# Attention feeding a gated MLP: the first stage ordered by a list scheduler, gate and value weights loaded once

## The chip, the cores and the metric

The kernel runs on one core of a Trainium2 chip. A core has five engines, each with its own instruction queue: TensorE (PE in the profile; its weight loads are PEld), VectorE (DVE), ScalarE (ACT), GpSimd (POOL) and SyncE (SP), which here issues the DMA transfers. The metric is the device time of one execution in microseconds, the median of several runs.

## The reference

```python
def sm_attn(qq, kk, vv):
    s = scale * np.matmul(qq, kk.transpose(0, 1, 3, 2))
    s = s - np.max(s, axis=-1, keepdims=True)
    a = np.exp(s)
    a = a / (np.sum(a, axis=-1, keepdims=True) + 1e-09)
    return np.matmul(a, vv)
q_d = q.reshape(B, H, Sd, factor, D).mean(axis=3)      # k_d, v_d likewise, factor = 4
out_up = np.repeat(sm_attn(q_d, k_d, v_d), factor, axis=2)
mask = np.abs(pos[:, None] - pos[None, :]) < factor
scores = np.where(mask, scale * np.matmul(q, k.transpose(0, 1, 3, 2)), -1000000000.0)
...                                                    # softmax of the scores, times v: out_local
x = (out_up + out_local).transpose(0, 2, 1, 3).reshape(B * S, H * D)
gate = 1.0 / (1.0 + np.exp(-(x @ w_gate)))
return gate * (x @ w_val) @ w_out
```

There are 8 batches of 8 heads, 576 positions and a head size of 64. The MLP has 4608 tokens, a model width of 512 and an inner width of 1536.

## The kernel before

**Attention.** Two heads of a batch form a unit, so there are 32 units, four to a batch. A unit loads four arrays (qk, qkd, v, vd), and its steps are: the pooled sums of q and k (prep2, GpSimd), the local scores s and the pooled scores sd (TensorE), their maxima, exponentials and sums, the transposes at and adt of the probabilities, their products with v (od for the pooled, x for the local part), and the sum of both, scaled (xs, VectorE), which is split into a high and a low half in f16 (xT, ScalarE and GpSimd). Units 0 to 7 (batches 0 and 1) keep their probabilities and v in f32, later units in f16 halves.

**MLP.** Tokens go in nine chunks of 512. For each of 12 slices of the inner width there is a gate product pg, a value product pv and an output product po, each of 12 matmuls of 128x512 in f16 (three products of halves for four pieces). A chunk needs the units of all its tokens: chunk 0 those of batch 0, chunk 1 those of batches 0 and 1.

**Weights.** They come as 64-bit words and are turned into two f16 halves on the chip. Each of 36 tiles (12 of each of wg, wv, wo, 512 KB each) is loaded twice. The first load (name ending in m) gives the absolute maximum (L160, VectorE), from which scales follow in two groups of slices; the second (ending in c) is converted in `wconv`: scaling on ScalarE (L213), a shift (L214), joining of the low bits (L215) and of the sign (L216) on VectorE, the high half on ScalarE (L222), the low half on GpSimd (L223). For wo both halves come from `split` (L164 ScalarE, L165 VectorE).

**Order.** The steps are put at positions by the numbers of the table `T`. Position 56 is the start of chunk 1; up to it the instructions are placed by the framework's scheduler in the order that its own estimates give, from there on TensorE keeps the order of the program. After that point a loop over chunks and slices issues gate, value and the output product of the slice before; a unit's steps are spread between them, and units are 9 positions (products) apart:

```python
    STEADY = dict(prep0=0, prep2=-3.5, s0=0, s1=0.1, sm=1.1, d0=2, dn=6.1, vd=9.4, v=8.2, a0=13, a1=13, at=14.4, od=15.6, x=16.6)
```

`awake` issues idle matmuls that keep TensorE active while it would wait. L413 is the line of every product, L491 the mask's addition to the local scores, L501 and L502 the maximum and its subtraction, L508 to L513 the sum and the division.

Of the kernel before, what the change touches and what calls it, by code (L numbers as in the profile page):

```python
# [19 lines left out]
T = dict(ma=4.5, mas=0.45, mb=9.5, mbs=0.5, c1=56, gs=2.66, g0=16.84, r1=1.99, rs=1.6, ob=3.16, v0=15.13, v1=16.62, v2=17.5, vs=2.12, o0=18, os=1.2, pro=2.36, u4=13.82, u5=21, u6=27, u7=32, l4=1.3, l5=2.77, l6=9.47, l7=8.68, lv=15.08, vm=1.58, b8=12, s8=9, hold=32.07, al=0.76, am=1, z=3.68, sd=0, sn=0.79, v0m=0.61, xd=[2, 3, 7], ad=[0, 3, 7], aa=[0, 1, 2, 3, 6], td=[0, 3, 9, 10], vd=[0, 1, 2, 3, 6, 9, 10], a_prep2=-0.89, a_s0=0.01, a_s1=0.52, a_sm=1.82, a_d0=2.39, a_dn=5.17, a_a0=4.37, a_vd=4.6, a_a1=5.1, a_v=2.74, a_at=5.22, a_od=5.79, a_x=8.38, m_prep0=-3.14, m_prep2=-1.43, m_s0=0.69, m_s1=2.59, m_sm=3.12, m_d0=2.84, m_a0=10, m_dn=10.78, m_vd=11.67, m_a1=12, m_v=13.07, m_at=13.44, m_od=15.64, m_x=17, k0=30, k_prep2=0, k_s0=2, k_s1=2, k_sm=4, k_d0=3, k_dn=0, k_a0=3, k_vd=8, k_a1=2, k_v=5, k_at=0, k_od=0, k_x=0)  # L20
# [22 lines left out]
TINY = 1e-30  # L43
EPS = 1e-9
NPC = NFC
WPC = DM
NWT = 1 + 2 * NPC
# [4 lines left out]
WAHEAD = 1  # L52
MAHEAD = 3
WGROUPS = [(0, 4), (4, NPC)]
SIGNBIT = -(1 << 31)
# [5 lines left out]
def attention_moe(ctx, tc, qk, qkd, v, vd, wg, wv, wo, mask, out):  # L61
# [23 lines left out]
    wg16 = cp.tile([P, NFC, 2, 4, P], F16, tag="wg16", name="wg16")  # L85
    wv16 = cp.tile([P, NFC, 2, 4, P], F16, tag="wv16", name="wv16")
# [7 lines left out]

    def borrow(i, n):
        taken[i] += n
        return room[i][:, NFC * WPC - taken[i] : NFC * WPC - taken[i] + n]

# [7 lines left out]
    def borrowed(eng, i, n):  # L106
        t = borrow(i, n * P)
        eng.memset(t, 0.0)
        return t.rearrange("p (a b) -> p a b", a=n)

    vplain = [borrowed(nc.vector, 0, NBLK), borrowed(nc.gpsimd, 0, NBLK)]
    vdblk = [zeroed(nc.gpsimd, [P, NKC, P], F32, f"vdblk{i}") for i in range(2)]
    ad = zeroed(nc.gpsimd, [QM, 2, NKC, 2, WIN], F32, "ad")
    vblk = cp.tile([P, 2, NBLK, P], F16, tag="vblk", name="vblk")
    flat = {id(vblk): vblk.rearrange("p t b c -> p (t b c)").bitcast(F32)}

    ones = cp.tile([P, 1], F32, tag="ones", name="ones")
# [781 lines left out]
```

## Time and profile before

| | |
|---|---|
| median of 3 runs | 1106.19 us (1105.46 to 1107.6) |
| profiled execution, its own time | 1106.37 us |
| its span | 1104.6 us |
| mean granted clock of TensorE | 0.956 |
| PE busy | 1047.4 us (95%) |
| DVE busy | 539.8 us (49%) |
| ACT busy | 476.6 us (43%) |
| POOL busy | 348.4 us (32%) |

The span runs from the first to the last instruction that the profile shows; the execution's own time is a little longer. Shares are means over the whole span; stages differ. The granted clock is given as a share of full speed (2.4 GHz).

### The profile page before, as it was taken

How to read it: one execution, taken by the hardware profiler on the slowest of the kernel's cores; microseconds unless marked ns; L12 is line 12 of the kernel's file. 1: busy time of each engine (PE TensorE's matmuls, PEld its weight loads, DVE VectorE, ACT ScalarE, POOL GpSimd, SP SyncE). 2: the span in 40 equal slices, each digit the busy share in tenths (PEclk: the TensorE clock that was granted, in tenths of full speed). 3: DMA queues.
4: the chain of work that ended last, by engine and by line, in shares of the span. 5: the costliest groups of instructions: out<-in, count | busy, mean ns of one | idle time of the engine just before them, and what ended most of it. 6: DMA issues, size and time to landing. Idle time of an engine off the chain costs nothing.

```text
span 1104.6 us, 18045 instructions
## 1 busy us (share of the span) xinstructions
PE 1047.4 (95%) x7267; PEld 546.4 (49%) x7267; DVE 539.8 (49%) x954; ACT 476.6 (43%) x1176; POOL 348.4 (32%) x348
## 2 busy tenths in 40 slices
PE   6877878988999999999999999999999999999998
PEld 4753334544555555555555555555555554444443
DVE  5779999855444444444444444444444322212112
ACT  5735566634444544454445444544444422122112
POOL 6424646633243334333433343333332200000000
PEclk8758989988999999999999999999999999999999
DMA  9977775422222322232223222321120000000001
GB/s 344 406 280 249 248 243 198 174 107 96 71 71 71 109 72 72 71 109 72 71 71 109 72 72 70 106 73 59 40 75 1 1 1 39 1 1 39 1 1 39
DMA packets 32083, 110.48 MB, mean 100 GB/s; under 512 B 3584, under 2 KB 3840, under 8 KB 32000
## 3 DMA queue, kind: packets, MB, share of 16 engines
q1 hardware_dynamic: 32000, 109.33, 28.4%
q8 instruction: 57, 0.93, 0.3%
q14 instruction: 26, 0.21, 0.1%
HBM read 99.88 MB, written 9.44 MB: 99 GB/s over the span
## 4 chain that ended last, share of the span: by engine, by line
PE 85%; DVE 7%; ACT 2%; DMA 2%; POOL 2%; issue 1%; SPq 0%; DVEq 0%; ACTq 0%
PE po L413 25%; PE pg L413 24%; PE pv L413 24%; PE x L413 4%; PE od L413 2%; PE at L571 2%; PE s L420 2%; PE sd L420 1%; PE adt L582 1%; DVE vdblk L404 1%; DVE wrv L216 1%; DVE hmx L160 1%; POOL wg L223 1%; POOL t L513 1%; ACT e L539 1%
## 5 line engine op out<-in xcount | busy, mean ns | idle before, releaser
L413 PE MATMUL pg<-xT,wg 128*128 128x512 f16 x1296 | 308.4, 387 | 9.2 <-ACT wg L222 4.6
L413 PE MATMUL pv<-xT,wv 128*128 128x512 f16 x1296 | 302.2, 382 | 5.3 <-ACT wv L222 3.7
L413 PE MATMUL po<-g,wo 128*128 128x512 f16 x1188 | 272.4, 379 | 0.0
L659 DVE SCALAR_TENSOR_TENSOR tanh<-tanh,pv 128x512 f32<-128x512 f32 x108 | 74.1, 686 | 344.9 <-PE pv L413 344.7
L413 PEld LDWEIGHTS <-wg 128*128 128x128 f16 x1296 | 124.9, 99 | 163.1 <-issue 14.5
L413 PEld LDWEIGHTS <-wv 128*128 128x128 f16 x1296 | 124.8, 98 | 151.8 <-issue 6.6
L413 PEld LDWEIGHTS <-wo 128*128 128x128 f16 x1296 | 125.3, 98 | 149.6 <-ACT wo L164 6.5
L651 ACT ACTIVATE tanh<-pg,tsc 128x512 f32<-128x512 f32 (+7 forms) x192 | 86.8, 496 | 194.9 <-PE pg L413 194.9
L667 ACT ACTIVATE g<-tanh,gs 128x512 f16<-128x512 f32 x99 | 71.5, 722 | 197.0 <-DVE tanh L659 197.0
L668 DVE SCALAR_TENSOR_TENSOR g<-tanh,gs,g 128x512 f16<-128x512 f32 x99 | 78.1, 789 | 40.8 <-ACT g L667 37.8
L502 POOL TENSOR_TENSOR t<-t,mx 128x768 f32<-128x768 f32 x32 | 47.9, 1497 | 108.9 <-DVE mx L501 108.9
L625 POOL TENSOR_TENSOR xT<-xs,xT 128x384 f16<-128x384 f32 (+7 forms) x54 | 53.7, 1011 | 55.6 <-ACT xT L623 55.6
L556 POOL TENSOR_TENSOR ad<-e,sme 72x288 f32<-72x288 f32 x52 | 34.6, 685 | 79.5 <-PE adt L582 76.3
L402 POOL TENSOR_TENSOR qkd<-qkd 128x576 f32<-128x576 f32 x29 | 34.9, 1203 | 62.4 <-DMA qkd<-in_qkd_dram 57.8
L402 POOL TENSOR_TENSOR vd<-vd 128x384 f32<-128x384 f32 x29 | 30.0, 1035 | 77.5 <-DMA vd<-in_vd_dram 77.5
L491 DVE SCALAR_TENSOR_TENSOR t<-s,mk 128x384 f32<-128x384 f32 x64 | 32.7, 550 | 44.3 <-PE s L420 38.1
L165 DVE SCALAR_TENSOR_TENSOR vblk<-v,svb,vblk 64x640 f16<-64x640 f32 x48 | 53.2, 1109 | 0.9 <-ACT vblk L164 0.2
L513 POOL TENSOR_TENSOR t<-t,sm 128x768 f32<-128x768 f32 x28 | 46.3, 1655 | 20.9 <-DVE sm L511 15.8
L404 POOL TENSOR_TENSOR vdblk<-vd 64x192 f32<-64x192 f32 x50 | 32.0, 640 | 50.5 <-PE od L413 48.6
L539 ACT ACTIVATE e<-sd,mxd 72x144 f32<-72x144 f32 x128 | 47.1, 371 | 1.8
L571 PE MATMUL at<-ident,t 128*128 128x128 f32 x192 | 30.7, 296 | 13.7 <-DVE t L513 5.0
L164 ACT ACTIVATE vblk<-v,svb 64x640 f16<-64x640 f32 x48 | 39.3, 819 | 0.8 <-DVE svb L157 0.2
(300 smaller groups left out, 1076.9 us busy)
## 6 DMA issues: line engine op xcount, KB each, us to landing
qk<-in_qk_dram SPq DMA_DIRECT2D x30, 610.0 KB, 3.9
qkd<-in_qkd_dram SPq DMA_DIRECT2D x29, 576.0 KB, 3.7
vd<-in_vd_dram SPq DMA_DIRECT2D x29, 384.0 KB, 3.0
v<-in_v_dram SPq DMA_DIRECT2D x32, 320.0 KB, 2.9
out_dram<-osb SPq DMA_DIRECT2D x16, 512.0 KB, 3.0
wo<-in_qk_dram SPq DMA_DIRECT2D x2, 610.0 KB, 10.1
wo<-in_qkd_dram SPq DMA_DIRECT2D x2, 576.0 KB, 9.4
out_dram<-osb SPq DMA_DIRECT2D x4, 256.0 KB, 2.0
```

The lines of the kernel that those rows point to most:

```text
L165: nc.vector.scalar_tensor_tensor(out=lo, in0=src, scalar=sc, in1=hi, op0=ALU.mult, op1=ALU.subtract)
L402: nc.gpsimd.tensor_tensor(out=x[:, :, 0:2], in0=x[:, :, 0:2], in1=x[:, :, 2:4], op=ALU.add)
L413: nc.tensor.matmul(o, w[a], x[c], start=first and i == 0, stop=last and i == len(pairs) - 1)
L502: nc.gpsimd.tensor_tensor(out=t, in0=t, in1=mx.unsqueeze(2).to_broadcast([P, 4 * NH, WIN]), op=ALU.subtract)
L513: eng.tensor_tensor(out=t, in0=t, in1=sm.unsqueeze(2).to_broadcast([P, 4 * NH, WIN]), op=ALU.mult)
L539: nc.scalar.activation(s["e"][:, qb, h, :], pt[:QM, qb * SD : (qb + 1) * SD], AF.Exp, bias=mx[:, qb : qb + 1], scale=QKSCALE / 16, accum_o ...
L571: nc.tensor.transpose(o, s["t"][:, par, i], ident)
L625: eng.tensor_tensor(out=x[:, hp, 1, o : o + n], in0=src, in1=x[:, hp, 0, o : o + n], op=ALU.subtract)
L651: nc.scalar.activation(t[:, o : o + n], pt[:, o : o + n], AF.Tanh, scale=tsc[:, b, fc : fc + 1])
L659: nc.vector.scalar_tensor_tensor(out=t, in0=t, scalar=1.0, in1=pt, op0=ALU.add, op1=ALU.mult)
L667: nc.scalar.activation(g[:, 0], t, AF.Copy, scale=gs[:, fc : fc + 1])
L668: nc.vector.scalar_tensor_tensor(out=g[:, 1], in0=t, scalar=gs[:, fc : fc + 1], in1=g[:, 0], op0=ALU.mult, op1=ALU.subtract)
```

## The change

The table `T` goes, with the framework's ordering of the first stage. Units 0 to 7, all weights and chunk 0 are described as small operations by `op` (engine, assumed duration, what they come after, which buffers they take and use). `order` gives every operation a latest start, backwards from the due times in `GOALS`, and then fills the engines in order of time: each takes, among the operations that are ready and whose buffers are free, the one with the earliest latest start. The result is issued in that order on all five engines; idle matmuls go where TensorE's list has a gap ahead of the first gate product.

```diff
+GOALS = {'x0': 23.22, 'x0s': 8.14, 'pv': 48, 'pvs': 7.76, 'x1': 105.9, 'x1s': 18.75, 'po': 139.42, 'pos': 2.17}
...
+WGROUPS = [(0, 2), (2, 4), (4, 8), (8, NPC)]
...
+    def order():
...
+            if k not in late:
+                o = ops[k]
+                end = min([goal.get(k, 400.0)] + [latest(x) - LAT[o["eng"]] for x in after[k]])
+                late[k] = end - o["us"]
...
+        by_eng = {g: sorted((k for k in ops if ops[k]["eng"] == g), key=lambda k: late[k]) for g in free}
...
+                    for k in by_eng[g]:
+                        o = ops[k]
+                        if any(end.get(a, 1e9) + LAT[ops[a]["eng"]] > now for a in o["after"]):
+                            continue
+                        got = places(o)
+                        if got is not None:
+                            break
...
+    seq, start, end, spare = order()
...
+    with tc.manual_schedule(engines={E.PE}):
+        with tc.manual_schedule(engines={E.DVE, E.Activation, E.Pool, E.SP}):
+            for k in seq:
+                if k in spare:
+                    awake(spare[k][1], spare[k][0])
+                ops[k]["f"]()
```

What is computed for the weights changes too. A gate or value tile is loaded once: its bits are joined in place in the slot behind its own in wg16 or wv16, its maximum is taken from the joined value (gate on ScalarE, value on VectorE), and both halves are made from it once its group's scale is known, the low one on VectorE. The sign and the scaling come from one ScalarE operation. There are four groups instead of two. wo tiles are still loaded twice.

```diff
-    def wconv(k, i, t, j):
...
-        nc.scalar.activation(h.bitcast(F32), h.bitcast(F32), AF.Copy, scale=hc[:, j : j + 1])
-        nc.vector.tensor_scalar(out=a, in0=h, scalar1=3, scalar2=None, op0=ALU.logical_shift_left)
-        nc.vector.scalar_tensor_tensor(out=a, in0=l, scalar=29, in1=a, op0=ALU.logical_shift_right, op1=ALU.bitwise_or)
-        nc.vector.scalar_tensor_tensor(out=a, in0=h, scalar=SIGNBIT, in1=a, op0=ALU.bitwise_and, op1=ALU.bitwise_or)
...
+    def wmant(k, i, n):
...
-            hi, lo = (dst[k][:, i, e] for e in range(2))
-            src = a.bitcast(F32).rearrange("p (c f) -> p c f", c=4)
-            nc.scalar.copy(hi, src)
-            nc.gpsimd.tensor_tensor(out=lo, in0=src, in1=hi, op=ALU.subtract)
...
+            f = wtile[k, i] = whole(k, i)
+        nc.scalar.activation(f, wtile[k, i, n][:, :, 1].bitcast(F32), AF.Prelu, scale=2.0 ** -112, alpha=2.0 ** 32)
+    def wshift(k, i):
+        a = wtile[k, i].bitcast(I32)
+        nc.vector.tensor_scalar(out=a, in0=a, scalar1=3, scalar2=None, op0=ALU.logical_shift_left)
+    def wjoin(k, i, n):
+        a = wtile[k, i].bitcast(I32)
+        nc.vector.scalar_tensor_tensor(out=a, in0=wtile[k, i, n][:, :, 0], scalar=29, in1=a, op0=ALU.logical_shift_right, op1=ALU.bitwise_or)
+    def wmax(k, i):
+        if k == "g":
+            junk = wk.tile([P, NKC * D * 4], F16, tag="junk", name=uniq("junk_g"), bufs=1)
+            nc.scalar.activation(junk[:, :WPC], wtile[k, i], AF.Abs, accum_out=hmx[:, col(k, i) : col(k, i) + 1])
...
+    def wlow(k, i):
+        hi, lo, src, sc = wparts(k, i)
+        nc.vector.scalar_tensor_tensor(out=lo, in0=src, scalar=sc, in1=hi, op0=ALU.mult, op1=ALU.subtract)
```

In units 0 to 7 the mask is added on TensorE (four matmuls with a scaled identity ahead of the scores), the maximum and its subtraction read the scores from PSUM on VectorE, and v is loaded straight into zeroed block-diagonal tiles, in pieces of 64 numbers, where ScalarE copied it before.

```diff
+    def load_vb(u):
+        vtile[u] = vflat[VTOF[u]]
+        for ps in HALVES:
+            nc.sync.dma_start(vtile[u][ps, :, ps], v[u][ps])
...
+        def scores():
...
+            for half_, ps in enumerate(HALVES):
+                for par, rows in enumerate(HALVES):
+                    nc.tensor.matmul(pts[par][ps, : 2 * NH * WIN], eye[rows],
+                                     mq[rows, half_].rearrange("p i c -> p (i c)"), start=True, stop=False)
+            mms = score_pairs(u, pts)
+            for i, (o, w, x) in enumerate(mms):
+                nc.tensor.matmul(o, w, x, start=False, stop=i >= len(mms) - 4)
...
+        def less(par):
+            m = s["mx"][:, 2 * NH * par : 2 * NH * (par + 1)].unsqueeze(2).to_broadcast([P, 2 * NH, WIN])
+            nc.vector.tensor_tensor(out=half(par), in0=of_bank(par), in1=m, op=ALU.subtract)
```

In the dense stage units start earlier and those of batch 2 are closer together:

```diff
-        return C1 - T["b8"] + (u - 2 * NPAIR) * T["s8"]
...
+        i = u - NPLAIN
+        return 7 * i - 1 if i < NPAIR else 9 * (i - NPAIR) + 27
...
+        for k in STEADY:
+            add(p0 + STEADY[k] - (2 if b == 2 and k in ("a0", "a1", "at", "od", "x") else 0), units[u][k])
+        add(base(u - 2) + STEADY["s0"] + 1, lambda u=u: load_qk(u))
+        add(base(u - 1) + STEADY["prep2"] + 1, lambda u=u: load_qkd(u))
+        add(base(u - 1) + STEADY["vd"] + 0.1, lambda u=u: load_vd(u))
```

VectorE before, at the place in the program where the middle weight tiles (slices 6 to 9) are worked on while chunk 0 runs (wg7c and the like are the second loads, hmx collects maxima, wrg and wrv the joined bits, vdblk the pooled v):

```order
L214 TENSOR_SCALAR wrv6_1293<-wv6c_1225 128x512
L214 TENSOR_SCALAR wrg7_1336<-wg7c_1302 128x512
L501 TENSOR_REDUCE mx_6_1409<-t_6_1370 128x12
L215 SCALAR_TENSOR_TENSOR wrv6_1293<-wv6c_1225,wrv6_1293 128x512
L215 SCALAR_TENSOR_TENSOR wrg7_1336<-wg7c_1302,wrg7_1336 128x512
L214 TENSOR_SCALAR wrv7_1373<-wv7c_1304 128x512
L160 TENSOR_REDUCE hmx_127<-wo9m_1333 128x1
L659 SCALAR_TENSOR_TENSOR tanh_0_5_1462<-tanh_0_5_1462,pv_0_5_1500 128x512
L216 SCALAR_TENSOR_TENSOR wrv6_1293<-wv6c_1225,wrv6_1293 128x512
L404 TENSOR_TENSOR vdblk0_114<-vd6_1616 64x3x64 x2
L216 SCALAR_TENSOR_TENSOR wrg7_1336<-wg7c_1302,wrg7_1336 128x512
```

VectorE in the changed kernel, after the last join of a gate tile, where the low halves of the later tiles are made and wo maxima taken (the numbers behind wo count its loads):

```order
L168 TENSOR_REDUCE hmx_128<-wo8_0_1438 128x1
L234 SCALAR_TENSOR_TENSOR wv16_114<-wv16_114,sw_130 128x512
L234 SCALAR_TENSOR_TENSOR wg16_113<-wg16_113,sw_130 128x512
L168 TENSOR_REDUCE hmx_128<-wo9_0_1455 128x1
L234 SCALAR_TENSOR_TENSOR wv16_114<-wv16_114,sw_130 128x512
L234 SCALAR_TENSOR_TENSOR wg16_113<-wg16_113,sw_130 128x512
L840 SCALAR_TENSOR_TENSOR xs_5_1552<-x_5_0_1551,sxb_136,od16_5_1499 128x464
L234 SCALAR_TENSOR_TENSOR wv16_114<-wv16_114,sw_130 128x512
L168 TENSOR_REDUCE hmx_128<-wo10_0_1476 128x1
L611 SCALAR_TENSOR_TENSOR tanh_0_8_1524<-tanh_0_8_1524,pv_0_8_1565 128x512
L168 TENSOR_REDUCE hmx_128<-wo11_0_1492 128x1
```

Low halves, which GpSimd made before, now stand on VectorE, the shift and one join of each tile stand earlier, and no sign step is left.

TensorE before, at the end of chunk 0, which is the start of chunk 1 (pg_1_0 is its first gate product, sd_8 the pooled scores of unit 8, x_7 the last product with v that chunk 1 needs):

```order
L423 MATMUL sd_8_1_2201<-qks_8_1962 72x144
L413 MATMUL od_7_2276<-adt16_7_2198,vdblk1_116 128x144 x3
L413 MATMUL x_7_0_2301<-at16_7_2024,vblk_120 128x58 x8
L413 MATMUL x_7_8_2312<-at16_7_2024,vblk_120 128x58 x2
L124 MATMUL mxt6_2337<-ident_103,vm1_2_2335 1x128
L413 LDWEIGHTS wg16_109
L413 MATMUL pg_1_0_2452<-xT1_506,wg16_109 128x512
```

TensorE in the changed kernel around the same x_7 (po_0 is the output product of chunk 0, g_0_10 and g_0_11 its last two slices):

```order
L403 MATMUL po_0_3_1770<-g_0_10_1759,wo16_115 128x512
L403 LDWEIGHTS wo16_115
L403 MATMUL po_0_3_1770<-g_0_10_1759,wo16_115 128x512
L403 MATMUL x_7_0_2097<-at16_7_2005,vring_123 128x58 x8
L403 MATMUL x_7_1_2107<-at16_7_2005,vring_123 128x58 x2
L403 LDWEIGHTS wo16_115
L403 MATMUL po_0_0_1767<-g_0_11_1837,wo16_115 128x512
```

The product x_7 stood inside the first gate product of chunk 1, and now stands ahead of the last output product of chunk 0; all twelve output products of chunk 0 now come after its last gate product. At later chunk starts the last unit's x, which stood four products ahead of the next chunk's gate product, now stands one output product ahead of it.

SyncE's queue of loads before, in the first stage (m and c are the first and second loads):

```order
L294 DMA vd6_1616<-in_vd_dram 128x768
L190 DMA wg8m_736<-in_wg_dram 128x1024
L190 DMA wv8m_782<-in_wv_dram 128x1024
L190 DMA wg9m_785<-in_wg_dram 128x1024
L190 DMA wg0c_788<-in_wg_dram 128x1024
L190 DMA wv9m_791<-in_wv_dram 128x1024
L190 DMA wv0c_813<-in_wv_dram 128x1024
L190 DMA wg10m_853<-in_wg_dram 128x1024
L190 DMA wv10m_855<-in_wv_dram 128x1024
```

SyncE's queue in the changed kernel at about the same place:

```order
L386 DMA vblk_122<-in_v_dram 64x10x64 x2
L363 DMA qk7_819<-in_qk_dram 128x1220
L371 DMA qkd6_862<-in_qkd_dram 128x1152
L197 DMA wg5_0_874<-in_wg_dram 128x1024
L355 DMA mk_108<-in_mask_dram 64x384 x4
L363 DMA qk8_2138<-in_qk_dram 128x1220
L379 DMA vd6_907<-in_vd_dram 128x768
L197 DMA wg6_0_913<-in_wg_dram 128x1024
L197 DMA wg7_0_928<-in_wg_dram 128x1024
L197 DMA wv4_0_936<-in_wv_dram 128x1024
L197 DMA wv5_0_960<-in_wv_dram 128x1024
```

Gate and value tiles appear once; vblk is a v block loaded in two transfers of 64x10x64 numbers, and qk8 of batch 2 stands among the loads of the first stage.

## Rows read from the trace of the kernel before

**Rows 1.** Windows: from:to, length, busy PE PEld DVE ACT POOL, clock, DMA share, GB/s.
```profile
0.00:262.00 262.00, 208.69 (x1468) 123.06 (x1469) 206.62 (x380) 144.10 (x352) 127.23 (x109) 0.82 0.67 242
262.00:1100.70 838.70, 838.69 (x5801) 423.38 (x5799) 332.73 (x574) 331.96 (x825) 221.14 (x239) 1.00 0.17 55
```
**Rows 2.** Windows of the first stage, the same columns.
```profile
0.00:60.00 60.00, 45.70 (x435) 36.81 (x436) 39.67 (x83) 36.69 (x112) 32.27 (x38) 0.76 0.93 357
60.00:80.00 20.00, 12.38 (x98) 9.82 (x98) 15.32 (x29) 5.62 (x11) 2.27 (x3) 0.50 0.84 300
80.00:160.00 80.00, 64.39 (x378) 29.95 (x377) 77.44 (x140) 45.61 (x101) 45.23 (x36) 0.88 0.76 260
160.00:230.00 70.00, 63.36 (x413) 33.12 (x412) 58.93 (x94) 43.73 (x88) 36.01 (x22) 0.93 0.47 166
```
**Rows 3.** Timeline of PE: chunk 0's first gate product, last output product (start, us).
```profile
77.02 1.04 PE L413 MATMUL pg<-xT,wg 128*128 128x512 f16 x2
...
229.53 0.59 PE L413 MATMUL po<-g,wo 128*128 128x512 f16 x2
```
**Rows 4.** Timeline of PE near the end of the dense stage.
```profile
1090.16 2.75 PE L413 MATMUL pg<-xT,wg 128*128 128x512 f16 x12
1092.76 2.75 PE L413 MATMUL pv<-xT,wv 128*128 128x512 f16 x12
```
**Rows 5.** Lines of PE, 262 to 1100.7 us: count, busy us, mean ns.
```profile
L413 PE MATMUL po<-g,wo 128*128 128x512 f16 x1152 | 264.1, 379 | 0.0
L413 PE MATMUL pv<-xT,wv 128*128 128x512 f16 x1140 | 261.8, 379 | 0.0
L413 PE MATMUL pg<-xT,wg 128*128 128x512 f16 x1128 | 259.1, 379 | 0.0
L413 PE MATMUL x<-at,vblk 128*128 128x58 f16 x720 | 23.4, 189 | 0.0
```
**Rows 6.** Timeline of DVE, 85 to 92.5 us.
```profile
85.74 0.68 DVE L216 SCALAR_TENSOR_TENSOR wrg<-wg1c,wrg 128x512 int32<-128x512 int32 x1
...
86.52 0.39 DVE L214 TENSOR_SCALAR wrv<-wv1c 128x512 int32<-128x512 int32 x1
...
89.70 1.89 DVE L216 SCALAR_TENSOR_TENSOR wrv<-wv1c,wrv 128x512 int32<-128x512 int32 x1
91.51 2.48 DVE L214 TENSOR_SCALAR wrg<-wg2c 128x512 int32<-128x512 int32 x1
```
**Rows 7.** Lines of DVE by shape, 0 to 262 us.
```profile
L165 DVE SCALAR_TENSOR_TENSOR wo<-wro,co,wo 128x512 f16<-128x512 f32 x12 | 11.4, 949 | 1.2 <-ACT wo L164 1.2
...
L501 DVE TENSOR_REDUCE mx<-t 128x12 f32<-128x768 f32 x10 | 9.5, 947 | 0.1
```
**Rows 8.** Timeline of POOL beside rows 6.
```profile
89.89 1.15 POOL L223 TENSOR_TENSOR wg<-wrg,wg 128x512 f16<-128x512 f32 x1
91.00 1.59 POOL L402 TENSOR_TENSOR qkd<-qkd 128x576 f32<-128x576 f32 x1
```
**Rows 9.** Windows of L214, L215 and L216 alone, in this order.
```profile
0.00:262.00 262.00, 21.98 (x36) 0.82 0.67 242
...
0.00:262.00 262.00, 31.64 (x36) 0.82 0.67 242
...
0.00:262.00 262.00, 29.70 (x36) 0.82 0.67 242
```
**Rows 10.** Lines of POOL by shape, 0 to 262 us.
```profile
L223 POOL TENSOR_TENSOR wg<-wrg,wg 128x512 f16<-128x512 f32 x12 | 16.9, 1412 | 37.6 <-ACT wg L222 37.6
...
L502 POOL TENSOR_TENSOR t<-t,mx 128x768 f32<-128x768 f32 x10 | 15.5, 1548 | 25.3 <-DVE mx L501 25.3
```
**Rows 11.** Window with the densest transfers, columns as in rows 1.
```profile
20.00:50.00 30.00, 24.46 (x184) 21.30 (x185) 20.40 (x46) 23.34 (x80) 14.24 (x14) 0.66 1.03 407
```
**Rows 12.** The page's DMA issues: count, KB each, us to landing.
```profile
v<-in_v_dram SPq DMA_DIRECT2D x32, 320.0 KB, 2.9
```
**Rows 13.** Timeline of all engines, 264 to 271 us: x of unit 8.
```profile
264.37 0.98 PE L413 MATMUL x<-at,vblk 128*128 128x58 f16 x30
...
268.26 1.98 POOL L625 TENSOR_TENSOR xT<-xs,xT 128x384 f16<-128x384 f32 x2 [1.55 <-ACT xT L623]
```

More of the change, by code (lines that the diff above doesn't have):

```diff
@@ new lines, in attention_moe, with mrows, mline, mspread @@
+    held = {}
+    def mrows(key, src, n):
+        pt = held[key] = bank(key, uniq("mxt"))
+        nc.tensor.transpose(pt[:n, :P], src(), ident)
+    def mline(key, n):
+        row = held[key, "row"] = wk.tile([n, 1], F32, tag="mxr", name=uniq("mxr"), bufs=4)
+        nc.vector.tensor_reduce(row, held[key][:n, :P], axis=AX.X, op=ALU.max)
+    def mspread(key, n):
+        pt = held[key]
+        nc.tensor.matmul(pt[:, 256 : 256 + n], held.pop((key, "row")).to_broadcast([n, P]), ident[:n, :n], start=True, stop=True)
+        held[key] = pt[:, 256 : 256 + n]
@@ L360, in attention_moe, with load_mask @@
     qkraw, qkdraw, vdraw = {}, {}, {}
+    def load_mask(dst_, rows, half, ps, par):
+        nc.sync.dma_start(dst_[ps, par], mask[rows, JHALF[half] : JHALF[half] + NH])
     def load_qk(u):
@@ L413, in product, with each @@
             nc.tensor.matmul(o, w[a], x[c], start=first and i == 0, stop=last and i == len(pairs) - 1)
-    def side_by_side(other, mms):
-        last = None if ordered else nc.tensor.matmul(other[:, 511:512], idle[:, :P], idle[:, :1], start=True, stop=True)
+    def each(mms):
         for o, w, x in mms:
-            if last is None:
-                nc.tensor.matmul(o, w, x, start=True, stop=True)
-                continue
-            with tc.issue_after(last.ins):
-                last = nc.tensor.matmul(o, w, x, start=True, stop=True)
-    ordered = []
+            nc.tensor.matmul(o, w, x, start=True, stop=True)
     owner = {}
@@ L679, in moe_out, with evict @@
             product(oacc[c][e], [wo16[:, fc, a, f] for a in range(2)], [g[:, a] for a in range(2)], fc == 0, fc == NFC - 1)
+    osb = {}
+    def evict(c, e):
+        if e % 2 == 0:
+            osb[c, e // 2] = raw.tile([P, 2, CH], F32, tag="stage", name=f"osb{c}_{e}", bufs=NST)
+        segs = segs_of_chunk(c)
+        if c == NCHUNK - 1 and e == 3:
+            segs = [(b, o + i * n // 2, n // 2) for b, o, n in segs for i in range(2)]
+        for i, (b, o, n) in enumerate(segs):
+            dst_, src = osb[c, e // 2][:, e % 2, o : o + n], oacc[c][e][:, o : o + n]
+            if e % 2 and i == 0:
+                nc.vector.tensor_scalar(out=dst_, in0=src, scalar1=osc[:, b : b + 1], scalar2=None, op0=ALU.mult)
+            else:
+                nc.scalar.activation(dst_, src, AF.Copy, scale=osc[:, b : b + 1])
@@ new lines, in store, with moe_gate, moe_val @@
+    def store(c, e):
+        if c == NCHUNK - 1:
+            nc.sync.dma_start(out[c, e // 2][:, e % 2], osb[c, e // 2][:, e % 2])
+        elif e % 2:
+            nc.sync.dma_start(out[c, e // 2], osb[c, e // 2])
+    def moe_gate(c, fc):
+        assert all(u in done for u in range(min(NU, -(-(c + 1) * CH // S) * NPAIR))), (c, fc)
+        gate_mm(c, fc)
+        gate_act(c, fc)
+    def moe_val(c, fc):
+        val_mm(c, fc)
+        val_mul(c, fc)
+        g_high(c, fc)
+        g_low(c, fc)
@@ L694, in moe_out, with op @@
-                if last:
-                    nc.sync.dma_start(out[c, e // 2][:, e % 2], osb[:, e % 2])
-                elif e % 2:
-                    nc.sync.dma_start(out[c, e // 2], osb)
-            del oacc[c]
+                evict(c, e)
+                store(c, e)
+            del oacc[c]
+    ops = {}
+    def op(name, eng, us, f, after=(), new=(), use=(), by=None):
+        assert name not in ops, name
+        ops[name] = dict(name=name, eng=eng, us=us, f=f, after=list(after), new=list(new), use=list(use), by=by)
```

833 lines of the change are left out of this document (515 added, 318 removed).

## The prediction

> **What bounds the kernel now.** I read first the busy time by stretch of the span [rows 1]. From 262 us to the last matmul at 1100.7 TensorE is busy for 838.69 of 838.70 us at a granted clock of 1.00: nothing on any other engine can shorten that stretch. Ahead of it lie 262 us in which TensorE is busy for 208.69 us at a clock of 0.82, and VectorE for 206.62 us. What the change can give lies there, since the products are the same in number before and after.
>
> The first stage splits up [rows 2]. Up to 60 us no engine is full: VectorE is idle for 20.3 us, transfers move 357 GB/s. From 60 to 80 the clock falls to 0.50. From 80 to 160 VectorE is busy for 77.44 of 80 us and TensorE for 64.39: VectorE bounds this piece. From 160 to 230 VectorE still has 58.93 of 70. The first gate product starts at 77.02 and the last output product of chunk 0 at 229.53 [rows 3], so chunk 0 takes 152 us for 36 products. In the dense stage a product starts every 92.76 - 90.16 = 2.60 us (2.59 over longer rows) [rows 4]: 36 would be 93 us.
>
> **The dense remainder, and the stage to be replaced.** From 262 us on there are 1,128 + 1,140 + 1,152 matmuls of twelve to a product, so 285 products, 738 us [rows 5]. The other 100.7 us of that stretch belong to the attention units: the product with v runs for 24 units (720 matmuls of 30), some operations of units 8 and 9 lie earlier, so about 23 units' worth, 4.4 us each. After the change the same dense code follows chunk 0: 288 products (8 chunks of 36) are 745.9 us, 24 units 105.7, and the span ends 3.9 us after the last matmul, 855.5 us in all. The span before is 1104.6, so its first stage is worth 249.1 us. The question is what the first stage takes when it is packed anew; call it T.
>
> **What goes, and what comes, on VectorE and GpSimd.** Per weight tile VectorE keeps the shift, one join (two before), and the absolute maximum, which for the 12 gate tiles goes to ScalarE; for the 24 gate and value tiles the low halves come to it from GpSimd. Undisturbed, the shift takes 0.39 us and the joining step 0.68, and one starts some 0.08 us before the end of the other (89.70 and 1.89 are 91.59, the next starts at 91.51) [rows 6]. The new subtraction of the low half has the shape of the wo one, 0.95 us [rows 7]. The local maximum and its subtraction now come as halves of 384 columns from PSUM, without the masking pass; the 768-column reduction is 0.95 [rows 7], so I price each half at 0.5.
>
> In the changed order batch 0 is done at row 92 of VectorE's list, the low half of the last gate tile (after which the last gate product can start) at row 219, the last low half at 288. With these prices and those of the unchanged small steps, the starts cover:
> - rows 1 to 92: 6 shifts, 6 joins, 3 low halves, 2 maxima of weights, 25 half-width maxima and subtractions, 8 full-width sums and multiplications, 42 small ones: 38 us clean.
> - rows 93 to 219: 19 shifts x 0.31, 19 joins x 0.60, 20 low halves x 0.87, 22 maxima x 0.59, 18 of the activation's products at about 0.68, some 6 us of small ones: 65 us clean.
> - rows 220 to 288: 11, 11, 13, and 6 of the activation's: about 32 us clean.
>
> Clean is the lower bound. Beside GpSimd the same shift took 2.48 us and a join 1.89 [rows 6], while GpSimd had two-input operations of its own running at 89.89 and 91.00 [rows 8]. The means before were 21.98/36 = 0.61 for the shift, 0.88 and 0.83 for the two joining steps [rows 9]: 0.2 us over clean each. At these means rows 93 to 219 cost 13 us more, 78. GpSimd loses the low halves (16.9 us twice) and most of the subtraction of the maximum (15.5 us for ten units) [rows 10]; it was busy for 81.2 of the 150 us from 80 to 230 [rows 2], 54%, and keeps about 32 us over a similar stretch, 25%. I take half of the excess: 71.5 us, and at the fill seen between 80 and 160 (97%) 74.
>
> The Trainium skill ("SBUF — State Buffer", section "SBUF: two separate sides") says that GpSimd and a VectorE operation with two inputs in SBUF, or in a two-port mode, exclude each other for a whole instruction. The 2.48 us agrees. By that rule the excess goes with GpSimd's busy time, as I take it; by row means alone the middle piece would be 6 us longer. The rule also speaks against the change, since the 24 low halves are now two-input operations on VectorE.
>
> **The three pieces of T.**
> - F, up to the end of batch 0. VectorE has 38 us, 41 with contention; the idle time before was 20.3 in the first 60 us [rows 2]. Four chains of units still stand behind one another, so I keep 19: 60 us. Bounds 52 (idle 12) and 70 (idle as before plus a late v, below).
> - G, from there to the last gate tile. VectorE 74. TensorE has 23 products, 59.6 us, and about 11 us of units 4 to 6: 70.6 at full clock, 76 to 80 at the 0.93 and 0.88 of [rows 2]. The two are about equal; I take 78. Bounds 71 (full clock, clean VectorE) and 90 (VectorE at its old means, with gaps).
> - E, the output products. In the new order all twelve output products come after the last gate product: gate 2.6, twelve output and one value product 33.7, units 6 and 7 with the new masking matmuls 10.9: 47 us, with VectorE at 32 to 44 beside it. Bounds 45 and 52. That is work put at the end, but TensorE is full there, so it is lost only in so far as G had room for it.
>
> T = 60 + 78 + 47 = 185 (168 to 212). The span becomes 855.5 + 185 = 1040.5; the profiled execution took 1106.37 for a span of 1104.6, 1.8 more, and stands 0.2 above the median of 1106.19, which I neglect. **1042 us**, 64 less than before; the bounds give 1025 to 1069.
>
> **Edits at nothing.** 24 loads of 512 KB go; transfers had a share of 0.47 to 0.93 [rows 2], about 45 MB remain, 110 us at the 407 GB/s seen between 20 and 50 us [rows 11], inside 185. If transfers were slower by two thirds they would bound T. The masking matmuls in bf16 (four of 384 columns for a unit) take at most 0.22 x 4 us a unit at the spacing of a 512-column matmul, and lie in F, where TensorE has room; without it 6 us. Scaling and sign in one ScalarE step replaces one of 0.8 us; ScalarE has about 140 us of work in 185.
>
> **The rivals.**
> - *Small pieces of v.* The v blocks of the first eight units are now loaded in pieces of 256 bytes. Below: 320 KB at 407 GB/s [rows 11], 0.8 us a unit. Above: two transfers a unit, each as long as the whole load's landing now, 2.9 us [rows 12], not overlapped: 5 us more for a unit, 20 for batch 0. F's own loads are 10 MB, 26 us, so two thirds of that show at most: 1042 + 13 = 1055. The pieces are needed last in a unit's chain, which speaks against it. The Trainium skill ("DMA: Bandwidth & Descriptors", section "Specifications") says that transfers below 512 bytes don't reach line rate; no run here shows how far.
> - *Crowding at chunk ends.* The last unit's product with v now stands one output product ahead of the next chunk's gate, at up to 6 chunk starts. From that product to the finished xT took 264.37 to 270.24, of which 4.9 us lie behind its end (265.35) [rows 13]; the output product and the gate's first nine matmuls cover 2.6 + 1.9 = 4.5. By the row 0.4 is missing; if VectorE or ScalarE is busy then, up to 2.5: 15 us, 1057.
> - *Everything packs.* Latencies hidden and the clock at 1.00: T = 168, 1025.
> - *Slower: the clock.* The work of chunk 0 and units 4 to 7 is 36 x 2.59 + 24 = 117 us of TensorE at full clock (the 24 an estimate: 4.4 a unit, 1.6 more for the masking matmuls and for v still in f32). If the packed stage has gaps that keep the clock at the 0.50 of 60 to 80 us [rows 2], it takes 234 us, T = 294, 1151 us. It decides from a mean clock below 117/(249 - 60) = 0.62 on. Against it: the clock stood at 0.88 and 0.93 with TensorE 80 and 90% busy, and the new order gives more of that.
>
> **How the numbers follow.** Main case 0.75 (its own range 1025 to 1069), small pieces 0.08, crowding 0.07, everything packs 0.07, the clock 0.03. I give the main time, 1042. The lower end is that of full packing; the upper takes the upper bound and a third of the crowding, 1074, leaving the clock and overlaps of mishaps outside. A measurement here tells 0.2%, 2.2 us, from no change: faster 0.95, same 0.01, slower 0.04 (the clock, and 0.01 for a stall that no row shows).
>
> **What would show it.** The first gate product near 60 us instead of 77; chunk 1's first gate near 185 instead of 230; VectorE or TensorE above 90% between; shifts near 0.4 us in the mean; from there on a product every 2.59 us with TensorE full. Wrong would be: TensorE waiting at chunk starts for xT, v landing after the probabilities, or a clock below 0.8 while chunk 0 runs.

## The result, and the profile after

The median fell from 1106.22 us to 1062.24 us (1060.13 to 1063.06, four runs), a ratio of 0.9598 with a 95% interval of 0.9581 to 0.9615: 44 us less, where 64 were forecast and a range of 1025 to 1074 was given. The profiled run took 1062.19 us, its span is 1060.4.

Windows of the changed kernel, cut at the events that the prediction names (columns as in [rows 1]):

```profile
0.00:60.00 60.00, 44.82 (x542) 36.54 (x542) 41.32 (x85) 35.74 (x110) 31.53 (x44) 0.76 0.97 299
60.00:68.30 8.30, 8.09 (x78) 7.51 (x79) 3.60 (x7) 3.32 (x7) 3.24 (x4) 0.50 1.02 334
68.30:149.90 81.60, 74.71 (x372) 37.34 (x372) 75.83 (x148) 57.78 (x133) 23.81 (x23) 0.94 0.76 266
149.90:200.80 50.90, 47.31 (x306) 25.63 (x305) 37.62 (x65) 27.23 (x64) 18.71 (x17) 1.00 0.34 106
200.80:1056.50 855.70, 852.46 (x5971) 431.82 (x5970) 345.53 (x602) 333.21 (x867) 233.40 (x250) 1.00 0.18 59
```

Timeline of TensorE in the changed kernel: the first gate product of chunk 0, its last one, and the first work of the dense stage:

```profile
68.30 4.16 PE L403 MATMUL pg<-xT,wg 128*128 128x512 f16 x10
...
149.91 2.76 PE L403 MATMUL pg<-xT,wg 128*128 128x512 f16 x12
...
200.80 0.93 PE L408 MATMUL s<-qk 64*64 64x64 f32 x48
```

So F, G and E of the prediction measured 68.3, 81.6 and 50.9 us instead of 60, 78 and 47, and the dense remainder 1060.4 - 200.8 = 859.6 instead of 855.5: 8.3 + 3.6 + 3.9 + 4.1 = 19.9 us, all of the gap between the forecast span of 1040.5 and the measured one. Against [rows 3], the first gate came 8.7 us earlier and chunk 0 took 133 us instead of 152.

The waits of TensorE in the first 200.8 us, longest first (engine, line, whom it waited for: us in total, times, longest):

```profile
PE s L728 <- DMA qk<-in_qk_dram: 4.8, 2, 3.1
PE pg L403 <- ACT wg L230: 3.4, 2, 2.9
PE s L724 <- DMA mq<-in_mask_dram: 2.4, 1, 2.4
```

Two of these three are for transfers, on which the prediction had put no term. A window of the changed kernel at the place of [rows 11]; then loads of v with count, KB each and us to landing, most of the half loads of the changed kernel and the whole ones of the first 262 us before:

```profile
20.00:50.00 30.00, 26.77 (x294) 22.84 (x298) 21.20 (x42) 17.81 (x60) 14.49 (x17) 0.65 0.98 283
```

```profile
vring<-in_v_dram SPq DMA_DIRECT2D x10, 160.0 KB, 8.2
```

```profile
v<-in_v_dram SPq DMA_DIRECT2D x14, 320.0 KB, 7.9
```

The transfer engines are as full as before (a share of 0.98, 1.03 in [rows 11]) and move 283 GB/s instead of 407. A half load of v takes 8.2 us to land. That says little of its form: the 2.9 us of [rows 12] are the median of a mostly quiet span, and a whole load in the busy first stage before took 7.9.

### The profile page after: what moved, and what is told of

Same layout as the page of the kernel before. It is cut to its first block, busy times and chain, and to the rows that moved or that the text cites. A ratio compares the mean times of both kernels' runs of the same rounds, so it can differ in the third digit from the quotient of the medians.

```text
span 1060.4 us, 17955 instructions
## 1 busy us (share of the span) xinstructions
PE 1027.4 (97%) x7264; PEld 538.9 (51%) x7264; DVE 504.4 (48%) x905; ACT 457.8 (43%) x1180; POOL 310.7 (29%) x338
## 4 chain that ended last, share of the span: by engine, by line
PE 87%; DVE 5%; DMA 4%; ACT 2%; issue 1%; POOL 1%; SPq 0%; DVEq 0%; POOLq 0%; ACTq 0%
PE pg L403 25%; PE pv L403 25%; PE po L403 24%; PE x L403 3%; PE od L403 2%; DMA qk<-in_qk_dram 2%; PE s L408 2%; PE sd L408 2%; PE at L526 1%; DMA wv<-in_wv_dram 1%; PE adt L540 1%; DMA wo<-in_wo_dram 1%; PE s L728 1%; DVE xs L840 0%; DVE wa L212 0%
## 5 line engine op out<-in xcount | busy, mean ns | idle before, releaser
L619 ACT ACTIVATE g<-tanh 128x512 f16<-128x512 f32 x99 | 62.4, 630 | 158.9 <-DVE tanh L611 158.9
L623 DVE SCALAR_TENSOR_TENSOR g<-tanh,g 128x512 f16<-128x512 f32 x99 | 75.0, 757 | 33.1 <-ACT g L619 32.3
L470 POOL TENSOR_TENSOR t<-t,mx 128x768 f32<-128x768 f32 x24 | 35.3, 1473 | 86.0 <-DVE mx L469 86.0
L173 DVE SCALAR_TENSOR_TENSOR vblk<-vring,svb,vblk 64x640 f16<-64x640 f32 x48 | 56.7, 1181 | 1.5 <-ACT vblk L172 0.7
L301 ACT ACTIVATE junk<-vring 128x640 f16<-128x640 f32 x28 | 20.5, 734 | 65.6 <-DMA vring<-in_v_dram 65.6
L172 ACT ACTIVATE vblk<-vring,svb 64x640 f16<-64x640 f32 x48 | 39.3, 819 | 11.2 <-PE x L403 8.1
L459 DVE SCALAR_TENSOR_TENSOR t<-s,mk 128x384 f32<-128x384 f32 x48 | 24.5, 552 | 40.6 <-PE s L408 40.6
L394 POOL TENSOR_TENSOR vdblk<-vd 64x192 f32<-64x192 f32 x44 | 23.8, 541 | 46.4 <-PE od L403 44.7
L481 POOL TENSOR_TENSOR t<-t,sm 128x768 f32<-128x768 f32 x22 | 32.4, 1472 | 14.6 <-DVE sm L479 14.6
L506 ACT ACTIVATE e<-sd,mxd 72x144 f32<-72x144 f32 x96 | 35.3, 371 | 1.5
```

What stands on the lines that cost most here:

```text
L172: nc.scalar.activation(hi, src, AF.Copy, scale=sc)
L173: nc.vector.scalar_tensor_tensor(out=lo, in0=src, scalar=sc, in1=hi, op0=ALU.mult, op1=ALU.subtract)
L470: nc.gpsimd.tensor_tensor(out=t, in0=t, in1=mx.unsqueeze(2).to_broadcast([P, 4 * NH, WIN]), op=ALU.subtract)
L506: nc.scalar.activation(s["e"][:, qb, h, :], pt[:QM, qb * SD : (qb + 1) * SD], AF.Exp, bias=mx[:, qb : qb + 1], scale=QKSCALE / 16, accum_o ...
L619: nc.scalar.activation(g[:, 0], tanh[c, fc], AF.Copy, scale=GSCALE)
L623: nc.vector.scalar_tensor_tensor(out=g[:, 1], in0=t, scalar=GSCALE, in1=g[:, 0], op0=ALU.mult, op1=ALU.subtract)
```

## The experiments

Twelve kernels ran, in three groups of four that share a chip and the runs of the kernel before. Medians of different groups differ by up to 2 us for the same kernel (before: 1105.7, 1103.93 and 1106.03 us), so the ratio is shown too. Each edit is made to the changed kernel unless another is named.

| run | median us | ratio to before, 95% interval | first gate | dense stage from |
|---|---|---|---|---|
| changed kernel | 1062.24 | 0.9598 (0.9581 to 0.9615) | 68.30 | 200.80 |
| e1_whole_v | 1060.96 | 0.9592 (0.9578 to 0.9606) | 65.08 | 197.13 |
| e2_x_earlier | 1062.41 | 0.9615 (0.9596 to 0.9634) | 66.43 | 199.21 |
| e4_load_twice | 1098.54 | 0.9933 (0.9917 to 0.9950) | 87.29 | 239.65 |
| e5_low_pool | 1065.49 | 0.9629 (0.9609 to 0.9650) | 67.72 | 203.79 |
| e6_v128_whole | 1055.09 | 0.9570 (0.9526 to 0.9614) | 60.25 | 192.63 |
| e7_v128_pieces | 1056.80 | 0.9573 (0.9551 to 0.9595) | 63.29 | 194.88 |
| e8_block_v | 1056.69 | 0.9571 (0.9555 to 0.9586) | 62.69 | 195.40 |
| e9_v128_twice | 1090.43 | 0.9881 (0.9865 to 0.9897) | 76.77 | 229.38 |
| e10_slot_only | 1070.63 | 0.9679 (0.9659 to 0.9700) | 68.67 | 209.42 |
| e11_after_again | 1059.29 | 0.9576 (0.9554 to 0.9598) | 66.37 | 199.92 |
| e12_best | 1052.74 | 0.9519 (0.9498 to 0.9539) | 60.02 | 192.68 |
| e13_s_later | 1058.93 | 0.9566 (0.9545 to 0.9588) | 63.59 | 197.44 |

The last two columns are start times in us in the one profiled run of each. Four of these kernels have the same first stage (the changed one, e2, e11, e13), and their first gate came between 63.59 and 68.30 us: what a single trace shows of F is good to some 5 us.

**Whole pieces of v on half the partitions.**

```diff
-            nc.sync.dma_start(vtile[u][ps, :, ps], v[u][ps])
+            nc.sync.dma_start(vtile[u].rearrange("p a b -> p (a b)")[ps, : NBLK * D], v[u][ps].rearrange("p a b -> p (a b)"))
```

> The v blocks of units 0 to 7 are loaded in the same two transfers a unit and at the same places of the queue, but each partition's 640 numbers go to one contiguous piece of 2,560 bytes instead of ten of 256 (so v does not lie block-diagonally, and the rows of batches 0 and 1 are not the reference's). Theory: the small pieces fill the transfer engines up to the end of batch 0 (283 GB/s at a share of 0.98 between 20 and 50 us against 407 before), so qk of unit 6 lands late; then 20 to 50 us move about 400 GB/s again, the first gate product starts at 60 to 62 us instead of 68.3, and the time falls by 6 to 8 us to 1054 to 1056. Rival: the first stage is bound by the chain of a unit's steps at the clock of 0.76, transfers only look full; then the first gate product stays within 2 us of 68.3 and the time falls by less than 2.

Measured: 1060.96 us. The window from 20 to 50 us of e1:

```profile
20.00:50.00 30.00, 26.67 (x351) 22.67 (x350) 23.78 (x48) 20.41 (x71) 14.87 (x18) 0.74 0.97 302
```

The rate is 302 GB/s, 19 above the changed kernel; but e2, e11 and e13, with the same loads as that kernel, show 293, 299 and 299, so one trace can't tell this from no change. The time fell by 1.3 us. The theory of the small pieces fell as stated. The rival's time came true, but its reason (only a chain of steps) isn't shown by that: the transfer engines are still full at a low rate, so something else in these loads may make them slow.

**v on all partitions.** Three forms: whole pieces, pieces of 256 bytes, and the block-diagonal form with its zeros, 640 KB a unit, from an input array vb of its own. In e1, e6, e7, e9 and e10 v does not lie block-diagonally, so the rows of batches 0 and 1 are not the reference's; these runs show the time alone.

```diff
-        for ps in HALVES:
-            nc.sync.dma_start(vtile[u][ps, :, ps], v[u][ps])
+        nc.sync.dma_start(vtile[u].rearrange("p a b -> p (a b)")[:, : NBLK * D], v[u].rearrange("p a b -> p (a b)"))   # e6
+        nc.sync.dma_start(vtile[u][:, :, :D], v[u])                                                                    # e7
+        nc.sync.dma_start(vtile[u], vb[u])                                                                             # e8, e12
```

> The v blocks of units 0 to 7 come in one transfer a unit to all 128 partitions, in contiguous pieces of 2,560 bytes (not block-diagonal, so the rows of batches 0 and 1 are not the reference's). Contiguous pieces on 64 partitions took the rate between 20 and 50 us only from 283 to 302 GB/s at a full share. Theory: what slows the transfers is that each of them fills only half of the partitions; then the rate between 20 and 50 us rises to about 400 GB/s as before, qk of unit 6 lands in time, the first gate product comes at 60 to 63 us and the time falls by 4 to 7 us to 1055 to 1058. Rival: the rate is low for another reason; then it stays near 300 GB/s and the time within 2 us of 1061, that of the contiguous halves.

> One transfer a unit to all 128 partitions, but in ten pieces of 256 bytes for each (the columns of the first head alone, so not the reference's values for batches 0 and 1). Theory (half the partitions cost, not the pieces): the rate between 20 and 50 us is within 20 GB/s of that with whole pieces on 128 partitions, and the time within 2 us of it. Rival (the pieces cost): the rate stays at 280 to 300 GB/s and the time at 1061 to 1063.

> v of units 0 to 7 lies block-diagonally with its zeros in an input array of its own, and comes in one transfer of 640 KB a unit to 128 partitions in pieces of 5,120 bytes: the reference's values, twice the bytes of v. Theory (half the partitions cost): rate near 400 GB/s, 1.6 MB more for the first five units are 4 us of transfers, so the first gate product at 62 to 65 us and the time 1056 to 1060. Rival (bytes or another cause): no rise of the rate, and the time 1062 to 1066.

Measured: 1055.09, 1056.80 and 1056.69 us. The windows from 20 to 50 us, of e6, e7 and e8:

```profile
20.00:50.00 30.00, 26.09 (x367) 21.80 (x367) 25.48 (x52) 21.98 (x77) 14.96 (x18) 0.88 0.82 310
```

```profile
20.00:50.00 30.00, 28.05 (x362) 24.15 (x362) 23.66 (x49) 21.30 (x74) 14.42 (x18) 0.76 0.92 309
```

```profile
20.00:50.00 30.00, 28.12 (x365) 24.34 (x365) 23.79 (x49) 21.59 (x75) 15.13 (x19) 0.77 0.93 368
```

Dividing the rate by the share tells how fast the engines are while they are busy. The changed kernel moves 283/0.98 = 289 GB/s for each full share (e2, e11 and e13, with the same loads, 299, 296 and 285), e1 302/0.97 = 311, e7 309/0.92 = 336, e6 310/0.82 = 378, e8 368/0.93 = 396, before 407/1.03 = 395. The literal expectation for e6, a rate near 400, was missed, since the engines now have spare time instead; that for e7 was met as worded (309 beside 310 GB/s, and 1.7 us), though for a full share e7 stands below e6. At whole pieces, all partitions instead of half of them are worth 311 to 378; at pieces of 256 bytes 289 to 336; on all partitions, whole pieces instead of small ones 336 to 378. Both matter, the half partitions more, by one trace of each. With v on all partitions (e6, e7, e8, e12) TensorE's waits for loads in the first 70 us sum to 3.2 to 4.3 us, in the five traces with the loads of the changed kernel (it, e2, e5, e11, e13) to 5.6 to 9.6; the first gate came at 60.02 to 63.29 us, and at 63.59 to 68.30. By the ratios the gain of e6 over the changed kernel is about 0.0028, 3 us, with intervals that overlap; by the medians 7, 1.8 of them the difference of the groups. The clean comparison is e12 against e13 below: on one chip, with v the only difference, 6.2 us.

**A second load of the weights.** An unread load of the same tile stands ahead of each load of a gate or value tile, in the changed kernel (e4), with v as in e6 (e9), and with an eighth of the bytes (e10, v as in e6). `order` made the sequence on all engines without these loads.

```diff
     def wload(k, i, n):
+        if k in "gv":
+            x = raw.tile([P, WPC, 2], I32, tag="stage", name=f"x{k}{i}", bufs=NST)
+            nc.sync.dma_start(x.rearrange("p a b -> p (a b)"), srcs[k][i].bitcast(I32))   # e10: [:, :128] of both
```

> Ahead of each load of a gate or value tile the same tile is loaded once more into another staging buffer that nobody reads: 24 loads, 12.6 MB, as many as the change took away, in the same order on all other engines. Theory (loads were a part of the gain): up to 80 us transfers are full, and each pair of loads ahead of the first gates delays them; 12.6 MB are 31 us at 407 GB/s, of which those of the first eight tiles show in full and the rest in part: plus 10 to 25 us, 1072 to 1087. Rival (the prediction's edit at nothing): from 68 us on transfers have a share of 0.76 and run ahead; plus less than 4 us.

> The loads of v on 128 partitions in whole pieces, together with the second, unread load of each gate and value tile that alone cost 36 us. Theory: the price of the 24 loads is their bytes at the rate that transfers reach, 12.6 MB at 400 GB/s, 31 us, where they are waited for; with the faster v the stage is less bound by transfers, so 15 to 28 us over the same kernel without the second loads. Rival: the 36 us come from queueing (a load waits for a staging buffer ahead of a unit's data on SyncE's queue), not from bytes; then 32 us or more again.

> As the kernel with v on 128 partitions and a second, unread load ahead of each gate and value tile, but the unread load brings only 512 of the 4,096 bytes of a partition (64 KB instead of 512 KB), into the same staging buffer. Whole unread loads cost 35 us over the same kernel without them. Theory: bytes are the price (12.6 MB at about 380 GB/s, 33 us, with a first stage that waits for loads throughout); an eighth of them costs 4 us or less, 1055 to 1060. Rival: the place in the ring of five staging buffers and in SyncE's queue is the price, whatever the load brings; then 15 us or more stay, above 1070.

Measured: 1098.54, 1090.43 and 1070.63 us. Against the kernels without the second loads that is 36 us (e4), 35 (e9) and 15.5 (e10; 12 by the ratios to before). The largest waits of TensorE in e4, in order of time:

```profile
59.99 1.56 PE L731 MATMUL s<-qk 64*64 64x64 f32 x48 [10.80 <-DMA qk<-in_qk_dram]
...
81.33 1.56 PE L731 MATMUL s<-qk 64*64 64x64 f32 x48 [8.11 <-DMA qk<-in_qk_dram]
...
97.12 1.01 PE L406 MATMUL pg<-xT,wg 128*128 128x512 f16 x2 [6.99 <-POOL xT L854]
```

The first two are the scores of units 4 and 6, which wait for their qk, and that stands behind the added loads on SyncE's queue: qk of unit 4 was issued at 54.81 us in e4, at 38.22 in the changed kernel. About half of the 36 us lie ahead of the first gate product (87.29 against 68.30), the other half in chunk 0. The waits of that queue in e9 (whom SyncE's issue waited for):

```profile
SPq L200 <- DMA xg<-in_wg_dram: 28.7, 8, 6.3
SPq L200 <- DMA xv<-in_wv_dram: 21.7, 6, 7.3
```

SyncE stands still until an unread load has landed, since only five staging buffers turn around. So neither theory holds alone: 12 to 15 us are the slot in the ring, the queue and the eighth of the bytes that e10 still loads; the other 20 or so are the rest of the bytes. The expectations for e4 (10 to 25 us) and e9 (15 to 28) were too low, and the one that I named the prediction's (under 4 us) far too low; e9 and e10 came out as their rivals had it.

**Low halves back on GpSimd.**

```diff
-        nc.vector.scalar_tensor_tensor(out=lo, in0=src, scalar=sc, in1=hi, op0=ALU.mult, op1=ALU.subtract)
+        if k == "o":
+            nc.vector.scalar_tensor_tensor(out=lo, in0=src, scalar=sc, in1=hi, op0=ALU.mult, op1=ALU.subtract)
+        else:
+            nc.gpsimd.tensor_tensor(out=lo, in0=src, in1=hi, op=ALU.subtract)
```

> The low halves of the 24 gate and value tiles are subtracted on GpSimd again, at the same places of the program (without the scale, so the low halves and the output are not the reference's). VectorE has 24 operations less, about 18 us, GpSimd 24 of 1.2 to 1.4 us more. Theory (TensorE, not VectorE, bounds the stretch from the first to the last gate product: 74.7 us of PE at clock 0.94 in 81.6): no gain, and longer shifts and joins beside GpSimd: the mean of the shift rises from 0.49 to about 0.6, the time stays within 2 us or rises by up to 6. Rival (VectorE bounds it, 75.8 of 81.6 us busy): the stretch falls by 4 us or more and the time with it.

Measured: 1065.49 us. The window from the first to the last gate product of chunk 0, and the shift's window by itself, in e5; then the shift (L208) and the join (L212) in the changed kernel:

```profile
67.70:153.00 85.30, 77.09 (x374) 37.76 (x374) 64.17 (x126) 58.49 (x135) 47.66 (x45) 0.92 0.73 256
...
0.00:205.00 205.00, 20.75 (x36) 0.88 0.71 235
```

```profile
0.00:201.00 201.00, 17.71 (x36) 0.88 0.72 238
...
0.00:201.00 201.00, 29.73 (x36) 0.88 0.72 238
```

VectorE lost 11.7 us of work there (75.83 to 64.17) and the stretch became longer, 85.3 us. TensorE's waits there are 8.1 us in e5, 2.1 of them for low halves that GpSimd now makes, and 6.9 in the changed kernel; even without those 2.1 the stretch would be no shorter. So relief of VectorE did not shorten G. GpSimd's work doubled (23.81 to 47.66) and the shift's mean went from 17.71/36 = 0.49 to 20.75/36 = 0.58 us.

**The waits in the dense stage.** From 200.8 us on TensorE waited only for this (the whole answer), and the first of the three in the timeline of the changed kernel:

```profile
PE x L403 <- DVE t L459: 3.2, 3, 1.8
```

```profile
240.19 0.93 PE L408 MATMUL s<-qk 64*64 64x64 f32 x48
242.96 0.97 PE L403 MATMUL x<-at,vblk 128*128 128x58 f16 x30 [1.84 <-DVE t L459]
```

The scores fill both banks of the attention's pair in PSUM, and x of the unit two before stands directly behind them, with no product of the MLP between.

```diff
-            add(p0 + STEADY[k] - (2 if b == 2 and k in ("a0", "a1", "at", "od", "x") else 0), units[u][k])
+            add(p0 + STEADY[k] - (3 if b == 2 and k in ("a0", "a1", "at", "od", "x") else 0), units[u][k])   # e2
+            late = u - NPLAIN in (2, 3, 4) and k in ("s0", "s1", "sm")                                         # e12, e13
+            add(p0 + STEADY[k] + late - (2 if b == 2 and k in ("a0", "a1", "at", "od", "x") else 0), units[u][k])
```

> The last five steps of the units of batch 2 stand one position earlier, so their product with v no longer comes directly behind the next scores. Theory: the three waits of x for VectorE's mask addition (1.84, 0.73 and 0.66 us at 242.96, 266.18 and 289.32) come from two products that need the same banks back to back; they go, and the time falls by 3 us to 1059. Rival: the bank is still wanted by another step, the waits move to it, and the time stays within 1 us.

> The changed kernel with only the scores of units 10, 11 and 12 one position later. Theory: the 3.2 us of waits of x go and nothing takes their place, 3 us under the changed kernel. Rival: waits of the transposes for ScalarE's exponentials appear in their place; within 1 us of the changed kernel.

Measured: 1062.41 us for e2. Its waits from the dense stage on, then those of e13:

```profile
PE at L526 <- ACT e L506: 3.2, 5, 1.2
PE mxt L143 <- DVE xs L565: 0.7, 1, 0.7
```

```profile
PE at L526 <- ACT e L506: 0.2, 1, 0.2
```

Moved earlier, x no longer waits, but the transposes wait 3.2 us for exponentials: the rival. With the scores later, the waits are gone, and the dense remainder is 1054.6 - 197.4 = 857.2 us against 859.6 in the changed kernel and 1061.1 - 199.9 = 861.2 in e11. The medians of e13 and e11, 1058.93 and 1059.29, can't tell this from no change, which is the time that e13's rival named, though its waits did not appear. That the later scores are worth their 2 to 4 us is shown by the traces alone: the remainder is 859.6 or some 861.2 us in all eleven traces without them, 857.2 in both with them (e12, e13).

**Both together.** e12 is e8 with the later scores of e13.

> The changed kernel itself, beside the next two on one chip: 1060 to 1063 us by its earlier runs.

> Block-diagonal v in whole transfers to 128 partitions, and the scores of units 10, 11 and 12 one position later, so that a product of the MLP stands between them and the product with v of the unit two before. Theory: the two gains add, 5 to 6 us from the first stage and 3 us from the three waits of x: 1052 to 1055, 8 us under the changed kernel. Rival: the later scores make the exponentials late and the transposes wait in their place, as when x was moved; then only the first gain stays, 1055 to 1058.

Measured: 1052.74 us beside 1059.29 for the changed kernel in the same group, a ratio to before of 0.9519 against 0.9576, the intervals apart. That is six and a half us. By the medians of this group 6.2 of them come with v (e12 against e13) and 0.4 with the later scores (e13 against e11). This version is faster than both kernels.

## Why the prediction was right in direction and in range, and 20 us too low

**What bounded the first stage.** The prediction took VectorE and TensorE as the two bounds and put the 24 loads under edits at nothing: "about 45 MB remain, 110 us at the 407 GB/s seen between 20 and 50 us, inside 185". For the new order that step failed: with the loads back (e4), 36 of the 44 us gained were gone. A mean over the stage hides when a load has to be there: up to 68 us the engines were full, and the queue on SyncE decides which unit's data come late. That the removal of these loads was itself most of the gain is not shown. In the kernel before, none of TensorE's waits in the first 262 us was directly for a load; among the longest were these, for the high half of a wo tile and for the local probabilities:

```profile
PE po L413 <- ACT wo L164: 5.7, 2, 2.9
PE at L571 <- DVE t L513: 5.0, 1, 5.0
```

VectorE was full from 80 to 160 us [rows 2], as the prediction had it. e4 adds the loads to a packed order that was made without them, so it shows what they cost there and not what they cost before. How the gain is shared between the scheduler, the lighter VectorE and the single load is not settled.

**F, 60 forecast, 68.3 measured.** Up to 68.3 us VectorE was busy for 44.9 us where 41 were taken, and idle for 23.4 where 19 were. The idle time was put down to chains; TensorE waited 4.8 us for qk in it. The longest of these waits, by the scores of unit 6, between the products with v of units 2 and 3:

```profile
52.31 2.38 PE L403 MATMUL x<-at,vblk 128*128 128x58 f32 x20
...
60.21 1.56 PE L728 MATMUL s<-qk 64*64 64x64 f32 x48 [3.06 <-DMA qk<-in_qk_dram]
...
63.98 4.52 PE L403 MATMUL x<-at,wg 128*128 128x58 f32 x20
```

From this wait to the first gate product the granted clock was 0.50, the lower of its two levels (1.2 GHz): the steps from these scores on took 8.1 us, the like ones before, from 49.98 to 54.59 us at a clock of 1.00, took 4.6. The wait and the clock together come to 6.6 of the 8.3 us. The rival of the small pieces named the place, but its 13 us were twice what the form of v is worth (6.2, e12 against e13), with its landing of 2.9 us taken from a quiet span; and it had a chance of 0.08 on the ground that the pieces are needed last in a unit's chain. What counted was not when v is needed but what stands behind it in the queue: qk of unit 6. The rival's mechanism was half right: pieces of 256 bytes cost, transfers to 64 partitions cost more (e1, e6, e7). With v on all partitions F was 60.02 to 63.29.

**G, 78 forecast, 81.6 measured.** TensorE's part was right: 74.71 us busy at a granted clock of 0.94, where 76 to 80 were taken at 0.88 to 0.93. That the two engines are about equal was not: with VectorE relieved the stretch did not shrink (e5), so TensorE and its 6.9 us of waits bound it, and for the waits the sum had no term; ScalarE (wg L230, 3.4 us) is the largest of those. VectorE's contention was sized well for the shift, 0.49 us against 0.50 by half of the excess, and badly for the joining steps, 29.73/36 = 0.83 against 0.78. Its busy time was forecast well: to the end of the last gate tile's low half, at 145.3 us, it was 71.2 us where 71.5 were forecast, in 77.0 us where 74 were. The last gate product started 4.6 us behind that, so it was not VectorE that held it.

The rule of the Trainium skill that the prediction weighed ("SBUF — State Buffer", section "SBUF: two separate sides") agrees with e5, where the shift took 0.09 us more in the mean beside more work on GpSimd; it did not decide the time.

**E, 47 forecast, 50.9 measured.** TensorE's work was 47.31 us as forecast. The 3.6 us above it are waits, 3.0 of them between the steps of units 6 and 7, for which the term had nothing. G and E together took 131.6 to 133.9 us in all nine traces without added loads and with the low halves on VectorE, whatever the form of v, where 125 were forecast. So these 7.5 of the 19.9 us remain in e12 too, which lies 10.7 us above the forecast.

**The dense remainder, 855.5 forecast, 859.6 measured.** The crowding rival looked at chunk starts; there was no wait at any. The three waits lie inside chunk 1, where units 7 positions apart put x directly behind scores, 3.2 us; the other 0.9 is not traced. The sum's 105.7 us for 24 units are themselves 0.6 more than its 100.7 us for 23 give.

**The clock.** In chunk 0 it was 0.94 and 1.00, so the rival of a slower kernel did not occur. Ahead of it the mean was 0.76 up to 60 us and 0.50 from there to 68.3, and F had no term for it. The same first stage met different clocks: with 0.83 up to 60 us the first gate came at 63.59 (e13), with 0.84 at 66.37 (e11), with 0.75 at 66.43 (e2), with 0.76 at 68.30.

## What to carry to other kernels

Price a load by the queue it stands in and by what stands behind it there, not by bytes against a mean rate: here 24 loads that the arithmetic hid cost 36 us when they were put back into the new order. When the share of the transfer engines is full, look at the rate per share: 283 GB/s at 0.98, beside 407 at 1.03 before, pointed to the form of the transfers, and e6 to e8 bore it out. Before calling an engine the bound because it is 93% busy, take work from it: G did not shrink when VectorE lost 11.7 us.

## What the runs showed of the hardware

Two loads to 64 partitions each in whole pieces let the stream of transfers move 311 GB/s for a full share (e1), one load to 128 partitions 378 (e6) and 381 (e9), with the same bytes of v; four traces with half loads in small pieces spread over 285 to 299. The stream as a whole slows, other loads included: in the first 68 us a load of qkd took 6.9 us to land in the changed kernel, 6.7 in e1 and 5.4 in e6. The Trainium skill ("SBUF — State Buffer", section "Door 1: The DMA port swizzle") says that a transfer's rate goes by how many ports its partitions reach, and (section "Can I just issue two DMAs to hit both halves?") that two transfers to the two halves don't make up for it; the 311 against 378 agree in direction, and the prediction had not drawn on it.
